# A gated recurrence in chunks: from seven levels of scores to one product with factored decays, the old way kept behind a branch

## The chip, the cores and the metric

The kernel runs on one core of one Trainium2 chip. Of the core's engines five appear in the profile: PE (TensorE: matrix products and transposes, with PEld for its weight loads), DVE (VectorE), ACT (ScalarE), POOL (GpSimd) and SP (SyncE, which issues the DMAs). The metric is the device time of one execution in microseconds. Before the change three timed executions took 1120.98 to 1123.78 us, median 1121.86.

## The reference

Two layers follow each other. The first is a gated linear recurrence, for 4 batches, 8 heads, 768 tokens and a head size of 48; the second mixes tokens through a rank of 32 and then channels through 1536 hidden ones.

```python
f = 1.0 / (1.0 + np.exp(-f_logit))
for t in range(S):
    state = f[:, :, t, :, None] * state + np.einsum('bhd,bhe->bhde', k[:, :, t], v[:, :, t])
    y[:, :, t] = np.einsum('bhd,bhde->bhe', q[:, :, t], state)
...
x = y.transpose(0, 2, 1, 3).reshape(B, S, H * D)
u = x + (x.transpose(0, 2, 1) @ U @ V).transpose(0, 2, 1)
out = u + np.maximum(u @ w_ch1, 0.0) @ w_ch2
```

Inputs q, k, v and f_logit are float32; f_logit is normal with mean 2 and deviation 0.5. The four weights arrive as float64 (their scale is a float64 number), and the kernel converts them to float32 on the chip from their bits.

## The kernel before, in words

Work goes in 16 *units*: a unit is two heads of one batch, one on partitions 0 to 47 and one on 64 to 111. The 768 tokens are cut into six chunks of 128. `attention(n, fill)` does a unit. PE transposes f, k and q (L182) so that channels lie on partitions and tokens along the free axis; ACT takes them out of PSUM, f with a sigmoid. Within a chunk the decay between two tokens is a product of f; it is built up in seven levels of a binary tree. On each level PE makes 12 score products `sc` of 64 columns (L231), DVE or ACT puts the part that belongs to the level into the score matrix A (L241 with a mask, L250 for the last two), DVE multiplies half of q (L253), POOL half of k (L256) by a neighbouring block's decay, and POOL forms the next level's block products (L261). The next level's scores wait for both. The diagonal comes from a product `dg` (L202). Then k is transposed back (L267), `ds` gives what each chunk adds to the state (L278), DVE runs the state from chunk to chunk (`st`, L286 and L288), and y is A times v plus q times state (L299, L301), copied by ACT into `x`.

`mixer(b)` makes a list of pieces for one batch: `low_rank` (`ph`, L317), six times `mix` (`pu` L324, the residual L325, and transposes `put` L331), and for each half of the tokens 12 times `ch1` (`pz`, L338, ReLU alternating between ACT and DVE) and three times `ch2` (`po`, L350, residual L353, and the store). The pieces of batch b are handed out as filler among the steps of the next batch's attention by `fill()`; those of the last batch stand alone at the end. During the first batch the filler is the weight conversion, `load_weight`, 32 tiles: a load into one of two `w_raw` buffers, one operation on ACT (L146), six on DVE (L147 to L153) and one on POOL (L154).

The program is recorded through a scheduler, which sets each engine's order by its own priorities; each engine then runs its list strictly in order, and so does SP's list of DMAs.

## Time and profile before

| | |
|---|---|
| timed executions | 1120.98, 1121.86, 1123.78 us |
| profiled execution, span from first to last instruction | 1124.9 us |
| own time of the profiled execution | given as the span alone; 1.1 us over the slowest timed one |
| PE busy | 1004.1 us, 89% |
| PEld / DVE / POOL / ACT busy | 726.0 / 334.8 / 266.0 / 144.2 us |
| batch 0 of attention, with the weight conversion | 0 to 252 us |
| batches 1, 2, 3, each with the mixer of the one before | 252 to 501, to 750, to 1003 us |
| last mixer, alone | 1003 to 1125 us |

In the group rows a name such as `sc<-qT,kT` is output and inputs by the program's tile names; behind it stand the shapes, the count of instructions, busy time, the mean in ns and the idle time before with what ended it. A float32 product on PE is two instructions. In timeline rows the first two numbers are the start and the length in us. The clock column is the TensorE clock that was granted, 1.00 being full.

### The profile page before, as it was taken

The page shows a single profiled execution, that of the slowest core. Times are in us where ns is not written, and L with a number is a line of the kernel's source. Part 1 is how long each engine was busy: PE and PEld are TensorE (multiplying, and loading weights), DVE is VectorE, ACT ScalarE, POOL GpSimd, SP SyncE. Part 2 cuts the span into 40 slices and gives each one's busy share as a digit, 9 for nine tenths or more (in the row PEclk, how much of TensorE's full clock was granted, in tenths as well). Part 3 has the DMA queues.
Part 4 walks back from the last instruction along what each step waited for, and adds up shares of the span by engine and source line. Part 5 has one row for each costly group of instructions (what it writes and reads, how often), then busy time and mean ns, then how long its engine had stood idle before and what let it go on. Part 6 is the DMA issues. An engine that isn't in the chain of part 4 may idle for free.

```text
span 1124.9 us, 13357 instructions
## 1 busy us (share of the span) xinstructions
PE 1004.1 (89%) x5592; PEld 726.0 (65%) x5592; DVE 334.8 (30%) x675; ACT 144.2 (13%) x269; POOL 266.0 (24%) x320
## 2 busy tenths in 40 slices
PE   5764748589999999999999999999999999988998
PEld 4654647576676767676766667576767667654555
DVE  3538585513223042213132142103132132101110
ACT  1111202011111111010111111010111111011000
POOL 4343533422131223022131223112131223100000
PEclk9999655556689898966689898965689998956999
DMA  9133423101030303010020302020020000000000
GB/s 129 29 82 85 99 70 76 38 11 32 1 43 1 56 8 43 15 39 11 1 43 8 57 1 43 22 43 1 1 43 8 15 1 1 22 1 0 8 15 21
DMA packets 108284, 34.29 MB, mean 30 GB/s; under 512 B 102016, under 2 KB 105088, under 8 KB 108224
## 3 DMA queue, kind: packets, MB, share of 16 engines
q1 hardware_dynamic: 108224, 33.44, 15.6%
q8 instruction: 44, 0.72, 0.3%
q14 instruction: 16, 0.13, 0.0%
HBM read 28.70 MB, written 4.72 MB: 30 GB/s over the span
## 4 chain that ended last, share of the span: by engine, by line
PE 81%; DVE 8%; POOL 6%; issue 3%; ACT 1%; POOLq 0%; DVEq 0%
PE sc L231 21%; PE po L350 17%; PE pz L338 14%; PE y L299 8%; PE y L301 7%; DVE A L241 5%; PE pt L182 4%; PE pu L324 3%; PE dg L202 2%; DVE qT L253 2%; POOL prod L261 2%; PE ph L317 2%; PE put L331 2%; POOL kT L256 2%; POOL qk L199 1%
## 5 line engine op out<-in xcount | busy, mean ns | idle before, releaser
L231 PEld LDWEIGHTS sc<-qT,kT 48*128 48x128 f32 x2688 | 226.2, 245 | 150.6 <-issue 91.1
L231 PE MATMUL sc<-qT,kT 48*128 48x64 f32 x2688 | 246.2, 336 | 86.0 <-DVE qT L253 63.0
L338 PE MATMUL pz<-uT,w 128*128 128x384 f32 x576 | 218.1, 524 | 0.8 <-ACT diag L205 0.8
L350 PE MATMUL po<-w,z 128*128 128x384 f32 x576 | 191.0, 489 | 0.0
L256 POOL TENSOR_TENSOR kT<-kT,prod 128x384 f32<-128x384 f32 x96 | 94.9, 989 | 356.6 <-PE sc L231 356.6
L241 DVE COPY_PREDICATED A<-mask,sc 128x384 f32<-128x384 int32 x160 | 110.6, 755 | 158.5 <-PE sc L231 157.4
L350 PEld LDWEIGHTS po<-w,z 128*128 128x128 f32 x576 | 108.4, 191 | 72.7 <-issue 0.3
L338 PEld LDWEIGHTS pz<-uT,w 128*128 128x128 f32 x576 | 110.0, 202 | 67.7 <-issue 9.8
L299 PE MATMUL y<-v_nat,A 128*128 128x48 f32 x384 | 99.9, 368 | 0.0
L301 PE MATMUL y<-st,qT 48*128 48x48 f32 x320 | 92.6, 381 | 0.3 <-DVE st L286 0.3
L299 PEld LDWEIGHTS y<-v_nat,A 128*128 128x128 f32 x384 | 78.8, 265 | 11.2
L301 PEld LDWEIGHTS y<-st,qT 48*128 48x128 f32 x320 | 68.7, 267 | 20.0 <-DVE st L288 4.9
L215 DVE TENSOR_TENSOR qT<-qT,fT 128x768 f32<-128x768 f32 x16 | 17.2, 1073 | 212.2 <-POOL qk L199 212.2
L253 DVE TENSOR_TENSOR qT<-qT,prod 128x384 f32<-128x384 f32 x96 | 55.4, 578 | 75.8 <-PE sc L231 75.8
L353 DVE TENSOR_TENSOR o<-x,po 128x384 f32<-128x384 f32 x24 | 13.3, 554 | 159.1 <-PE po L350 159.1
L209 POOL TENSOR_TENSOR A<-ident,diag 128x768 f32<-128x768 f32 x32 | 46.5, 1473 | 47.8 <-ACT diag L205 47.8
L261 POOL TENSOR_TENSOR prod<-fT 128x384 f32<-128x384 f32 x16 | 13.2, 826 | 183.2 <-ACT fT L190 180.0
L344 ACT ACTIVATE z<-pz 128x384 f32<-128x384 f32 x48 | 23.6, 491 | 240.3 <-PE pz L338 240.3
L250 ACT COPY A<-sc 32x384 f32<-32x384 f32 (+1 forms) x48 | 27.7, 577 | 189.5 <-PE sc L231 189.3
L342 DVE TENSOR_SCALAR z<-pz 128x384 f32<-128x384 f32 x48 | 26.6, 555 | 75.3 <-PE pz L338 75.3
L199 POOL TENSOR_TENSOR qk<-qT,kT 128x768 f32<-128x768 f32 x16 | 28.9, 1804 | 53.2 <-ACT qT L192 53.2
L202 PEld LDWEIGHTS dg<-halves,qk 128*128 128x128 f32 x192 | 27.8, 226 | 17.4 <-POOL qk L199 14.6
(57 smaller groups left out, 638.4 us busy)
## 6 DMA issues: line engine op xcount, KB each, us to landing
w_raw<-in_moe_w_ch_dram SPq DMA_DIRECT2D x24, 384.0 KB, 3.2
f_nat<-in_f_logit_dram SPq DMA_DIRECT2D x32, 144.0 KB, 3.0
k_nat<-in_k_dram SPq DMA_DIRECT2D x32, 144.0 KB, 3.4
q_nat<-in_q_dram SPq DMA_DIRECT2D x32, 144.0 KB, 3.9
v_nat<-in_v_dram SPq DMA_DIRECT2D x32, 144.0 KB, 3.8
out_dram<-o SPq DMA_DIRECT2D x24, 192.0 KB, 1.9
w_raw<-in_moe_U_dram SPq DMA_DIRECT2D x6, 32.0 KB, 1.7
w_raw<-in_moe_V_dram SPq DMA_DIRECT2D x2, 96.0 KB, 2.0
```

The costliest lines, as they stand in the source:

```text
L182: nc.tensor.transpose(pt[:, c // (NCH // 2), (c % (NCH // 2)) * C : (c % (NCH // 2) + 1) * C], nat[n % NSLOT][nm][:, c].rearrange("p h d - ...
L199: nc.gpsimd.tensor_tensor(qk, T["q"], T["k"], ALU.mult)
L202: nc.tensor.matmul(dg[:, 2 * c : 2 * c + 2], lhsT=qk[:, chunk[c]], rhs=halves, start=True, stop=True)
L209: nc.gpsimd.tensor_tensor(A[:, par], ident.unsqueeze(1).broadcast_to((P, NCH, C)), diag[:, :, par : par + 1].broadcast_to((P, NCH, C)), AL ...
L231: nc.tensor.matmul(sc[:, par, c * HC : (c + 1) * HC], lhsT=T["k"][r, chunk[c]], rhs=qv[r, c * nbc : (c + 1) * nbc, 1, :], start=True, stop ...
L241: nc.vector.copy_predicated(A[:, par].rearrange("p c (n two h) -> p (c n) two h", two=2, h=half)[:, :, 1, :], masks[l].unsqueeze(1).broadc ...
L253: nc.vector.tensor_tensor(qv[:, :, 1, :], qv[:, :, 1, :], bv[:, :, 0:1].broadcast_to((P, nb, half)), ALU.mult)
L256: nc.gpsimd.tensor_tensor(kv[:, :, 0, :], kv[:, :, 0, :], bv[:, :, 1:2].broadcast_to((P, nb, half)), ALU.mult)
L299: nc.tensor.matmul(o, lhsT=A[:, par, c, :], rhs=vt[:, c, par, :], start=True, stop=(c == 0))
L301: nc.tensor.matmul(o, lhsT=T["q"][r, chunk[c]], rhs=st[r, c, :], start=False, stop=True)
L338: nc.tensor.matmul(pm[:, 0:HALF], lhsT=w1[:, m, i * P : (i + 1) * P], rhs=uT[a][:, m, :], start=(m == 0), stop=(m == NDC - 1))
L350: nc.tensor.matmul(pm[:, 0:DM], lhsT=z[a, i][:, s * P : (s + 1) * P], rhs=w2[:, i, :], start=(i == 0), stop=(i == NFC - 1))
```

## The change

The kernel gets a new main path, `factored_path`, and keeps the old one as `general_path`, which runs behind a branch at the end when a flag says that the new one's range did not suffice.

The new path loads f, k and q so that a partition holds 24 tokens of 48 channels in one run of 1136 numbers, for 32 channels with some overlap, and turns 32 x 32 blocks on DVE. Decays are factored: X is the product of f from a token to the chunk's end (a scan backwards along the tokens), Y is the product from the chunk's start to a token divided by the whole chunk's (a scan forwards that begins each chunk with the reciprocal). k is multiplied by X and q by Y on POOL, so one score product of 128 columns for each chunk and head gives all pairs, and a causal mask on DVE takes them into A. `ds`, the states and y's state part are done for both heads in one product, with a mask `own` that clears what belongs to the other head. The smallest product of each chunk is kept, and the flag `ok` says whether all are at least 1e-18.

Work on a unit is cut in pieces: `attend(n)` (scores, kept, scores, states, read) and, interleaved with it, `prepare(n + 1)` (gates, keep, keys, read, queries), with filler after each. In the mixer a tile is now transposed (`turn`) after the next one's `mix`, and ReLU is on ACT alone. In the conversion ACT's operation is gone, and POOL has one more.

```diff
-        low, head, m = tmp(F32, "w_low"), tmp(U32, "w_head"), tmp(F32, "w_m")
-        nc.scalar.activation(low, lo, AF.Copy, scale=2.0**-52)
+        head, m = tmp(U32, "w_head"), tmp(F32, "w_m")
...
-        nc.vector.scalar_tensor_tensor(m, head, 2.0**-20, low, ALU.mult, ALU.add)
+        nc.vector.scalar_tensor_tensor(m, lo, 2.0**-32, head, ALU.mult, ALU.add)
...
+        nc.gpsimd.tensor_scalar(m, m, 2.0**-20, None, ALU.mult)
         nc.gpsimd.tensor_tensor(dst, m, s.bitcast(F32), ALU.mult)
...
-            if i % 2:
-                nc.vector.tensor_relu(out=z[a, i], in_=pm[:, 0:HALF])
-            else:
-                nc.scalar.activation(z[a, i], pm[:, 0:HALF], AF.Relu)
+        nc.scalar.activation(z[a, i], pm[:, 0:HALF], AF.Relu)
...
-        todo = [low_rank] + [lambda t=t: mix(t) for t in range(NCH)]
+    todo = [low_rank]
+    for t in range(NCH):
+        todo.append(lambda t=t: mix(t))
+        if t:
+            todo.append(lambda t=t: turn(t - 1))
+    todo.append(lambda: turn(NCH - 1))
...
+def factored_path(ctx, tc, q, k, v, f_logit, moe_U, moe_V, moe_w_ch1, moe_w_ch2, out, ok):
...
+    raw = [{nm: const.tile([P, W], F32, name=f"{nm}_raw{i}") for nm in "fkq"} for i in range(2)]
...
+                    nc.sync.dma_start(
+                        out=dst[p0 : p0 + rows, :],
+                        in_=bass.AP(head.tensor, head.offset + part * NB, [[TB * D, rows], [1, W]]),
+                    )
...
+    def turned(t, src_tile):
+        nc.vector.transpose(
+            t.rearrange("p (i c) -> p c i", c=TB),
+            bass.AP(src_tile.tensor, src_tile.offset, [list(src_tile.ap[0]), [D, TB], [1, NB]]),
+        )
...
+        def gates():
+            fT = one.tile([P, S], F32, name="fT")
+            turned(fT, r["f"])
+            fv = fT.rearrange("p (c t) -> p c t", t=C)
+            nc.scalar.activation(by_chunk[:, :, 1:C], fv[:, :, 1:C], AF.Sigmoid)
+            f0 = T["f0"] = two.tile([P, NCH], F32, name="f0")
+            nc.scalar.activation(f0, fv[:, :, 0], AF.Sigmoid)
+        def keep():
+            X = T["X"] = one.tile([P, S], F32, name="X")
+            nc.vector.tensor_tensor_scan(
+                backwards(X, S - 1, S), backwards(f, S, S), backwards(ends, S - 1, S), 0.0,
+                ALU.mult, ALU.add,
+            )
+            X0 = X.rearrange("p (c t) -> p c t", t=C)[:, :, 0]
+            nc.vector.tensor_copy(least[:, n, :], X0)
...
+            nc.vector.tensor_single_scalar(X1, X0, LEAST, ALU.max)
+            nc.vector.reciprocal(e.rearrange("p (c t) -> p c t", t=C)[:, :, 0], X1)
...
+            nc.vector.tensor_tensor(whole, T["f0"], X0, ALU.mult)
+        def keys():
...
+            turned(kT, r["k"])
+            nc.gpsimd.tensor_tensor(kT, kT, T["X"], ALU.mult)
+        def read():
...
+            nc.vector.tensor_tensor_scan(Y, f[:, 0:S], e, 0.0, ALU.mult, ALU.add)
+        def queries():
...
+            turned(qT, r["q"])
+            nc.gpsimd.tensor_tensor(qT, qT, T["Y"], ALU.mult)
+            if n + 2 < NU:
+                load_unit(n + 2)
...
+        def scores(g):
...
+            for c in range(G):
+                for par in range(2):
+                    nc.tensor.matmul(
+                        sc[:, par, c * C : (c + 1) * C],
+                        lhsT=T["k"][rows[par], chunk[g * G + c]],
+                        rhs=T["q"][rows[par], chunk[g * G + c]],
+                        start=True, stop=True,
+                    )
+            for par in range(2):
+                nc.vector.tensor_tensor(
+                    T["A"][:, par, g * G : (g + 1) * G, :],
+                    sc[:, par, 0 : G * C].rearrange("p (c i) -> p c i", i=C),
+                    causal.unsqueeze(1).broadcast_to((P, G, C)),
+                    ALU.mult,
+                )
...
+        def states():
...
+                nc.tensor.matmul(
+                    ds[:, c * PW : (c + 1) * PW], lhsT=T["kb"][:, c, :],
+                    rhs=vt[:, c].rearrange("p h d -> p (h d)"), start=True, stop=True,
+                )
...
+            nc.gpsimd.tensor_tensor(
+                st, dn, T["whole"][:, 1:NCH].unsqueeze(2).broadcast_to((P, NCH - 1, PW)), ALU.mult
+            )
+            for c in range(2, NCH):
+                nc.vector.scalar_tensor_tensor(
+                    st[:, c - 1, :], st[:, c - 2, :], T["whole"][:, c : c + 1], st[:, c - 1, :],
+                    ALU.mult, ALU.add,
+                )
...
+                if c:
+                    nc.tensor.matmul(o, lhsT=T["q"][:, chunk[c]], rhs=T["st"][:, c - 1, :],
+                                     start=True, stop=False, skip_group_check=True)
+                for par in range(2):
+                    nc.tensor.matmul(o[:, par * D : (par + 1) * D], lhsT=T["A"][:, par, c, :],
+                                     rhs=vt[:, c, par, :], start=(c == 0), stop=True,
+                                     skip_group_check=True)
...
+    nc.vector.tensor_single_scalar(ok, lowest, LEAST, ALU.is_ge)
+    for f in todo:
+        f()
...
+    good = nc.values_load(ok[0:1, 0:1], min_val=0, max_val=1)
+    with tc.If(good == 0):
+        with ExitStack() as inner:
+            general_path(inner, tc, *args)
```

The scheduler sets the order anew. PE, a unit of batch 0 before the change, from its scores to the first y with a state (names as in the section on the kernel before):

```order
L202 MATMUL dg<-halves,qk 128x2 x6
L231 MATMUL sc<-qT,kT 128x64 x84
L267 MATMUL pt<-ident,kT 128x128 x5
L299 MATMUL y<-v_nat,A 128x48 x3
L182 MATMUL pt<-ident,f_nat_122 128x128 x3
L278 MATMUL ds<-v_nat,kb 64x48 x10
```

The same on PE in the changed program, unit 0:

```order
L308 MATMUL sc<-qT,kT 128x128 x6
L325 MATMUL pt<-ident,kT 128x128 x5
L308 MATMUL sc<-qT,kT 128x128 x6
L334 MATMUL ds<-v_nat,kb 128x96 x5
L362 MATMUL y<-v_nat,A 128x48 x2
L359 MATMUL y<-st,qT 128x96
```

The scores went from 84 products to two groups of six, and the transposes of f, k and q and the diagonal have left PE.

DVE in the changed program, unit 3 of batch 0: masks into A (L315) and states (L349) among the weight conversion (L46 to L53), with the numbers of the tiles:

```order
L53 SCALAR_TENSOR_TENSOR w_s_423<-w_raw_415,w_e_421 128x384
L315 TENSOR_TENSOR A_924<-sc_925,causal_106 128x384
L48 SCALAR_TENSOR_TENSOR w_m_443<-w_raw_440,w_head_442 128x384
L50 TENSOR_SCALAR w_e_446<-w_raw_440 128x384
L315 TENSOR_TENSOR A_924<-sc_986,causal_106 128x384
L51 TENSOR_SCALAR w_e8_447<-w_e_446 128x384
L315 TENSOR_TENSOR A_924<-sc_986,causal_106 128x384
L52 TENSOR_SCALAR w_e_446<-w_e8_447 128x384
L339 TENSOR_TENSOR dn_1004<-ds_998,own_109 128x480
L53 SCALAR_TENSOR_TENSOR w_s_448<-w_raw_440,w_e_446 128x384
```

A mask that waits for PE now stands between two steps of a conversion; before, the level's mask L241 and the product L253 stood in such places, seven times a unit.

PE in the changed program, from the low-rank step of batch 0's mixer to unit 4's scores (ph L73, pu L80, put L89):

```order
L73 MATMUL ph<-x,U 32x384 x6
L80 MATMUL pu<-h,V 128x384 x2
L89 MATMUL put<-ident,x 128x128 x3
L80 MATMUL pu<-h,V 128x384
...
L80 MATMUL pu<-h,V 128x384
L308 MATMUL sc<-qT,kT 128x128 x6
L325 MATMUL pt<-ident,kT 128x128 x5
```

Units 0 to 3 stand ahead of it without filler on PE, since the filler of batch 0 is conversion; unit 4's scores stand behind most of the low-rank step, and batch 0's pz behind unit 4's.

More of the change, by code (lines that the diff above doesn't have):

```diff
@@ L346, in ch2 @@
-        def ch2(a, s):
-            t = a * TPH + s
-            pm = ps_mm.tile([P, 512], F32, name="po", tag="mm")
-            for i in range(NFC):
-                nc.tensor.matmul(pm[:, 0:DM], lhsT=z[a, i][:, s * P : (s + 1) * P], rhs=w2[:, i, :],
-                                 start=(i == 0), stop=(i == NFC - 1))
-            o = three.tile([P, DM], F32, name="o")
-            nc.vector.tensor_tensor(o, x[:, t, :], pm[:, 0:DM], ALU.add)
-            nc.sync.dma_start(out=out[b, t * P : (t + 1) * P, :], in_=o)
@@ L356, in mixer @@
-        todo = [low_rank] + [lambda t=t: mix(t) for t in range(NCH)]
-        for a in range(2):
-            todo += [lambda a=a, i=i: ch1(a, i) for i in range(NFC)]
-            todo += [lambda a=a, s=s: ch2(a, s) for s in range(TPH)]
-        return todo
+        return mixer_pieces(nc, b, x_tiles[b], U, V, w1, w2, ident, out, two, three, zp, ps_mm)
     FILLS = NL + 3
@@ L380, with kernel @@
         f()
+@with_exitstack
+def kernel(
+    ctx: ExitStack,
+    tc: tile.TileContext,
+    q: bass.AP,
+    k: bass.AP,
+    v: bass.AP,
+    f_logit: bass.AP,
+    moe_U: bass.AP,
+    moe_V: bass.AP,
+    moe_w_ch1: bass.AP,
+    moe_w_ch2: bass.AP,
+    out: bass.AP,
+):
+    nc = tc.nc
+    args = (q, k, v, f_logit, moe_U, moe_V, moe_w_ch1, moe_w_ch2, out)
+    flag = ctx.enter_context(tc.tile_pool(name="flag", bufs=1))
+    ok = flag.tile([1, 1], I32, name="ok")
+    with ExitStack() as inner:
+        factored_path(inner, tc, *args, ok)
+    good = nc.values_load(ok[0:1, 0:1], min_val=0, max_val=1)
+    with tc.If(good == 0):
+        with ExitStack() as inner:
+            general_path(inner, tc, *args)
 _INS = ['q', 'k', 'v', 'f_logit', 'moe_U', 'moe_V', 'moe_w_ch1', 'moe_w_ch2']
```

302 lines of the change are left out of this document (241 added, 61 removed).

## The prediction

> **What bounds the kernel now.** I read the page's head first, then a table of five stretches (one for each batch of attention, and the last mixer), then the chain of waits.
>
> ```profile
> span 1124.9 us, 13357 instructions
> PE 1004.1 (89%) x5592; PEld 726.0 (65%) x5592; DVE 334.8 (30%) x675; ACT 144.2 (13%) x269; POOL 266.0 (24%) x320
> DVE  3538585513223042213132142103132132101110
> ```
> ```profile
> core 0: us, PE busy (x) PEld busy (x) DVE busy (x) ACT busy (x) POOL busy (x), PEclk, DMA share, GB/s
> 0.00:252.00 252.00, 164.99 (x1074) 148.20 (x1074) 134.35 (x303) 38.94 (x73) 96.14 (x123) 0.74 0.35 69
> 252.00:501.00 249.00, 240.52 (x1400) 170.97 (x1399) 62.30 (x116) 32.06 (x59) 57.46 (x68) 0.83 0.14 25
> 501.00:750.00 249.00, 240.70 (x1399) 170.97 (x1399) 62.47 (x116) 32.07 (x59) 57.46 (x68) 0.83 0.14 25
> 750.00:1003.00 253.00, 244.28 (x1393) 173.31 (x1393) 62.31 (x116) 31.82 (x59) 54.90 (x61) 0.81 0.07 14
> 1003.00:1125.00 122.00, 113.61 (x330) 62.59 (x330) 13.35 (x24) 9.31 (x20) 0.00 (x0) 0.91 0.03 10
> ```
> The last line of the head has DVE in 40 slices of 28 us. Two regimes. From 252 us on, PE is busy 97% of the time: what counts is its number of instructions. In the first 252 us nothing is full: PE and DVE take turns, with the weight conversion (DVE) between them. The chain says the same:
>
> ```profile
> by line: PE sc L231 20.8%; PE po L350 16.8%; PE pz L338 14.1%; PE y L299 7.6%; PE y L301 7.0%; DVE A L241 4.7%; PE pt L182 3.8%; issue 2.7%; PE pu L324 2.6%; PE dg L202 2.5%; DVE qT L253 1.9%; POOL prod L261 1.8%; PE ph L317 1.7%; PE put L3
> ```
> Scores, y, dg and pt, that is attention, hold most of PE's part; the mixer's pz and po come next. The prices on PE (a float32 product counts as two instructions, a transpose as one):
>
> ```profile
> L231 PE MATMUL sc<-qT,kT 48*128 48x64 f32 x2688 | 246.2, 336 | 86.0 <-DVE qT L253 63.0 <-POOL kT L256 16.7 <-DVE w_head L147 5.0
> L338 PE MATMUL pz<-uT,w 128*128 128x384 f32 x576 | 218.1, 524 | 0.8 <-ACT diag L205 0.8
> L350 PE MATMUL po<-w,z 128*128 128x384 f32 x576 | 191.0, 489 | 0.0
> L324 PE MATMUL pu<-h,V 32*128 32x384 f32 x48 | 35.7, 841 | 0.6 <-ACT h L320 0.6
> L331 PE MATMUL put<-ident,x 128*128 128x128 f32 x72 | 20.8, 423 | 4.3 <-DVE x L325 4.3
> L317 PE MATMUL ph<-x,U 128*32 128x384 f32 x48 | 19.8, 570 | 0.7 <-ACT x L304 0.7
> L267 PE MATMUL pt<-ident,kT 128*128 128x128 f32 x80 | 16.2, 351 | 9.4 <-POOL kT L256 9.4
> L278 PE MATMUL ds<-v_nat,kb 128*64 128x48 f32 x320 | 16.3, 263 | 0.0
> ```
> I use busy time over count, not the mean: the records overlap. The mixer is 218.1 + 191.0 + 35.7 + 20.8 + 19.8 = 485.4 us of PE and is kept. In the middle batches it takes 121 of 249 us, so attention takes 128, or 32 per unit. The change works on those 32.
>
> **The change, part by part.** Gone are seven levels of scores with their masks and waits, the diagonal, and 18 transposes per unit on PE. Now PE does per unit 12 score products, 5 transposes, 5 ds products and 17 for y. DVE takes over transposes and gains two scans. So the first stretch becomes DVE's, the rest stays PE's, and I sum the two apart.
>
> *Stage 1, DVE, until unit 5's last state.* The order shows why it ends there: PE's scores for units 4 and 5 stand behind DVE's transposes, which stand among the conversions; the last conversions lie between unit 5's states.
>
> ```profile
> L353 DVE TENSOR_TENSOR o<-x,po 128x384 f32<-128x384 f32 x24 | 13.3, 554 | 159.1 <-PE po L350 159.1
> L215 DVE TENSOR_TENSOR qT<-qT,fT 128x768 f32<-128x768 f32 x16 | 17.2, 1073 | 212.2 <-POOL qk L199 212.2
> L288 DVE SCALAR_TENSOR_TENSOR st<-st,prod,ds 128x48 f32<-128x48 f32 x64 | 16.8, 263 | 2.0
> L147 DVE TENSOR_SCALAR w_head<-w_raw 128x384 uint32<-128x384 uint32 (+2 forms) x32 | 13.1, 408 | 3.1 <-DMA w_raw<-in_moe_w_ch_dram 3.0
> L148 DVE SCALAR_TENSOR_TENSOR w_m<-w_head,w_low 128x384 f32<-128x384 uint32 (+2 forms) x32 | 15.5, 486 | 4.0 <-POOL w L154 2.2 <-ACT w_low L146 1.3 <-POOL U L154 0.3
> L150 DVE TENSOR_SCALAR w_e<-w_raw 128x384 uint32<-128x384 uint32 (+2 forms) x32 | 18.3, 573 | 0.1
> L151 DVE TENSOR_SCALAR w_e<-w_e 128x384 uint32<-128x384 uint32 (+2 forms) x32 | 12.2, 382 | 0.3
> L152 DVE TENSOR_SCALAR w_e<-w_e 128x384 uint32<-128x384 uint32 (+2 forms) x32 | 11.0, 343 | 0.4
> L153 DVE SCALAR_TENSOR_TENSOR w_s<-w_raw,w_e 128x384 uint32<-128x384 uint32 (+2 forms) x32 | 19.8, 620 | 0.5
> L152 DVE TENSOR_SCALAR w_e<-w_e 128x32 uint32<-128x32 uint32 x6 | 1.1, 181 | 0.2
> ```
> Conversion: 13.1 + 15.5 + 18.3 + 12.2 + 11.0 + 19.8 = 89.9 us. A unit: four score masks of 384 from PSUM at 0.554 (L353's shape), 2.22; one of 480, 0.69; four state steps at 0.263, 1.05; four operations on six numbers at 0.18, what 32 numbers cost in the last row, 0.72. Neither a 32x32 transpose nor a scan is in the trace. The nearest row has the same 768 elements, L215 at 1.07. A transpose I bound by ACT's 768-wide copy (0.80, below) and twice 1.07, and take 1.07. A scan has two inputs as L215 has, and each output needs the one before: 1.07 to 2.15, and I take the middle, 1.6. Unit: 4.68 + 3 x 1.07 + 2 x 1.6 = 11.1 us (9.2 to 15.4); six units 67.
>
> [...]
>
> Between, DVE waits:
>
> ```profile
> 4.66 1.51 PE L182 MATMUL pt<-ident,f_nat 128*128 128x128 f32 x6 [4.66 <-DVE mask_f L85]
> 39.52 2.83 PE L231 MATMUL sc<-qT,kT 48*128 48x64 f32 x24 [1.67 <-DVE w_head L147]
> 47.88 1.33 PE L267 MATMUL pt<-ident,kT 128*128 128x128 f32 x5 [1.35 <-POOL kT L256]
> ```
> ```profile
> L199 POOL TENSOR_TENSOR qk<-qT,kT 128x768 f32<-128x768 f32 x16 | 28.9, 1804 | 53.2 <-ACT qT L192 53.2
> L192 ACT COPY kT<-pt 128x768 f32<-128x768 f32 x16 | 12.8, 799 | 26.6 <-PE pt L182 26.6
> w_raw<-in_moe_w_ch_dram SPq DMA_DIRECT2D x24, 384.0 KB, 3.2
> ```
> The first gates land at about 5 us (4.66 before, for half the bytes). From the last query transpose to the first mask DVE waits for POOL's product (1.8) and six score products on a cold PE (12 instructions, 1.4 at 2.83 / 24, more for twice the columns: 2.1); the second half then waits for five transposes and six products less two masks (1.33 + 2.1 - 1.1); ds about 0.8: 7 us. Units 0 to 2 have little conversion to fill it: 21 us. In units 3 to 5 conversions stand in the gaps, but a mask row waits in order with conversions queued behind it: 4 each, 12. On SP a w_raw load waits for one of two buffers, and the next unit's inputs stand behind it; it lands in 3.2 us, about one conversion: 5 us of waits. The residual adds: 6 x 0.55 = 3.3. **Stage 1: 5 + 67 + 90 + 21 + 12 + 5 + 3 = 203 us.**
>
> *Stage 2, PE.* In stage 1 PE has done ph, pu and put of one batch (76.3 / 4 = 19) and 24 of 288 pz products (18): 485.4 - 37 = 448 us are left, the exposed last mixer included. Ten units are left.
>
> ```profile
> 486.03 1.35 PE L299 MATMUL y<-v_nat,A 128*128 128x48 f32 x6
> 560.37 0.66 PE L299 MATMUL y<-v_nat,A 128*128 128x48 f32 x2
> 603.56 0.77 PE L299 MATMUL y<-v_nat,A 128*128 128x48 f32 x6
> ```
> Scores: 24 instructions between L231's 246.2 / 2688 = 0.092 and twice that for twice the columns: 2.2 to 4.4, middle 3.3. Transposes 16.2 / 16 = 1.0. Ds: half the instructions, each twice as wide both ways: from 16.3 / 16 = 1.0 to ten at the slow 128-row price above (1.35 / 6 = 0.225), 2.3; middle 1.7. y: 34 instructions, all on 128 rows. Alternating with 48-row products one costs 0.33 on a slow clock (0.66 for two); in a run of their own 0.225, or 0.77 / 6 = 0.13 fast. Nearest is the fast run, since pz stands around it: 0.145, 4.9 in all. **Unit 10.9 (8.6 to 19), ten units 109.**
>
> Waits: the level-to-level stalls (86 us at L231) have nothing left to wait for. What is late next is y, for the states: ds 1, DVE's 0.7, POOL's 480 of 768 elements at 1.8, and four steps of 0.26, together 4 us, while three to nine pz products (0.64 each, below) cover 2 to 6. I leave 1 us a unit, 10; behind a late y stand PE's next pz, and nobody waits for those but ACT. The last mixer idles 122.0 - 113.6 = 8.4; turning a tile after the next mix takes off some 3: 5. ReLU, now all on ACT, hides under the 1.9 us of products that make a tile; uncovered it costs 0.4 a tile (half of L192's 768). The input loads double in bytes but are issued a unit ahead, and hide under that unit's 11 us of DVE or more; uncovered, a landing is 3 to 4 us. At the end each engine loads the flag and jumps over the other path: 0 to 10 (three landings of 3.2), and I take 4, near one.
>
> **Sum: 203 + 448 + 109 + 15 + 4 = 779 us** against the profiled span of 1124.9; the median, 1121.86, lies 3 below it, so 776.
>
> **The rivals.**
> - *PE stays fast* (0.22). pz and po carry slow stretches: the last mixer's run shows the price without them.
>
> ```profile
> 1051.81 23.38 PE L350 MATMUL po<-w,z 128*128 128x384 f32 x72
> 560.00:566.00 6.00, 6.00 (x22) 5.09 (x22) 0.00 (x0) 0.00 (x0) 0.00 (x0) 0.50 0.00 0
> ```
>  72 instructions in 23.2 us is 0.3225 each, 371.5 for 1152 against 409.1. The clock halves in the long y runs (0.50 at 560); shorter ones may not reach it. Saved: 36 on pz and po, 23 with units at 8.6, 11 on DVE with 9.2, and half of stage 1's waits, 16: 690. Against it: ph and pu remain. [...]
> - *DVE is dearer* (0.17). Transposes and scans at 2.15 give 15.4 a unit, 26 more; w_raw waits that nothing hides, 1.6 (half of 3.2) for each of 24 tiles, 38: 840. For it: six new large operations without a row; against: DVE before waited only 3.1 for such loads.
> - *PE stays slow in attention* (0.06): 19 a unit, 81 more, and pz and po lose their 38 twice: 895. The 0.50 at 560 speaks for it, the 0.8 of every stage above against it.
> - *The other path runs too* (0.02). If a product of 127 gates falls below 1e-18, the whole old program follows: 776 + 1122 = 1898, slower. Worked out from the reference's inputs the smallest is 7.9e-10, so only a fault in the flag would do it; then the change would not do what it says either.
>
> **How the numbers follow.** Forecast 0.53, rivals 0.22, 0.17, 0.06, 0.02. The range, 690 to 855, holds the forecast's own bounds, most of the dearer-DVE case and the slower half of the fast one; 0.2 stays outside. Below 0.3% (3.4 us) this measurement tells nothing apart. Only the last rival is not faster: faster 0.97, same 0.01, slower 0.02.
>
> **What would show it.** Stage 1: DVE near 80% busy up to about 200 us, a unit's own work near 11 us, scans at 1.6. Stage 2: PE over 95% busy, a y run of 17 products near 5 us, middle batches of about 165 us. The end: 122 us or a little less from the last x to the end, then under 10 us of jumps. Wrong, if PE waits for DVE after 250 us, if one scan or transpose costs over 2.2, or if L536 appears.

## The result, and the profile after

The changed kernel takes 722.62 us (median of four runs, 721.53 to 724.5); the kernel before, timed beside it, 1122.82. The ratio is 0.6434, with an interval of 0.6413 to 0.6455: 1.55 times as fast. The forecast was 776 us, 53 above the time; the range of 690 to 855 holds it.

The head of the page after, with DVE's 40 slices (now of 18 us each):

```profile
span 719.6 us, 6593 instructions
PE 614.4 (85%) x2489; PEld 403.6 (56%) x2489; DVE 336.6 (47%) x539; ACT 98.1 (14%) x205; POOL 143.5 (20%) x123
DVE  6668798999984566254553542354211201000000
```

PE has lost 390 of its 1004 us, 200 of them at the scores (`sc` has 45.9 us, L231 had 246.2); DVE has lost none. The table of stretches, cut where unit 5's last y product ends and where the last sum ends (columns as before the change: length, then busy time and count of PE, PEld, DVE, ACT and POOL, the granted clock, the DMA share and GB/s):

```profile
0.00:211.00 211.00, 116.25 (x527) 91.31 (x528) 173.80 (x316) 22.64 (x47) 97.39 (x93) 0.85 0.49 117
211.00:713.00 502.00, 498.16 (x1964) 312.26 (x1963) 162.41 (x224) 75.48 (x158) 46.12 (x30) 0.94 0.19 45
713.00:719.00 6.00, 0.00 (x0) 0.00 (x0) 0.36 (x1) 0.00 (x0) 0.00 (x0) 0.80 0.11 38
```

The two stages are there as forecast: DVE busy 82% of the first 211 us, PE 99% of the rest, and then some 6 us of end. What differs is the price of the second stage, which its groups show (first the 211 to 713 us of PE alone, then three of DVE's dearest over the whole run):

```profile
L105 PE MATMUL po<-w,z 128*128 128x384 f32 x576 | 188.7, 487 | 0.0
L96 PE MATMUL pz<-uT,w 128*128 128x384 f32 x528 | 182.0, 498 | 0.0
L362 PE MATMUL y<-v_nat,A 128*128 128x48 f32 x243 | 39.3, 289 | 0.0
L308 PE MATMUL sc<-qT,kT 48*128 48x128 f32 x240 | 26.1, 325 | 0.0
L80 PE MATMUL pu<-h,V 32*128 32x384 f32 x36 | 22.8, 737 | 0.8 <-ACT h L76 0.6 <-DVE x L81 0.2
L89 PE MATMUL put<-ident,x 128*128 128x128 f32 x54 | 14.8, 400 | 2.1 <-DVE x L81 2.1
L73 PE MATMUL ph<-x,U 128*32 128x384 f32 x36 | 12.1, 487 | 0.6 <-DVE o L108 0.6
```
```profile
L237 DVE STREAM_TRANSPOSE fT<-f_raw 128x768 f32<-128x768 f32 x16 | 33.3, 2079 | 6.4 <-DMA f_raw<-in_f_logit_dram 4.4 <-DMA out_dram<-o 1.9
L261 DVE TENSOR_TENSOR_SCAN X<-fz,ends 128x768 f32<-128x768 f32 x16 | 28.1, 1757 | 26.0 <-ACT fz L255 20.4 <-ACT f L257 5.3
L48 DVE SCALAR_TENSOR_TENSOR w_m<-w_raw,w_head 128x384 f32<-128x384 uint32 (+2 forms) x32 | 21.8, 680 | 2.5 <-POOL w L55 2.2 <-POOL U L55 0.2
```

The mixer's five lines take 188.7 + 182.0 + 22.8 + 14.8 + 12.1 = 420.4 us of the second stage; what is left of PE's 498.2 is attention: 77.8 us, 7.8 for each of ten units. (Records overlap where one product follows another; here the overlap is counted with the mixer.) One unit's y run, from the timeline (start, length):

```profile
251.72 0.54 PE L362 MATMUL y<-v_nat,A 128*128 128x48 f32 x4
252.09 0.43 PE L359 MATMUL y<-st,qT 128*128 128x96 f32 x2
252.36 0.57 PE L362 MATMUL y<-v_nat,A 128*128 128x48 f32 x4
...
255.44 4.10 PE L96 MATMUL pz<-uT,w 128*128 128x384 f32 x12
```

From the first y to the next pz pass 3.72 us: 0.11 for each of the 34 instructions, at a granted clock of 1.00.

### The profile page after: what moved, and what is told of

It is laid out like the page before. It is cut to its first block, busy times and chain, and to the rows that moved or that the text cites. A ratio compares the mean times of both kernels' runs of the same rounds, so it can differ in the third digit from the quotient of the medians.

```text
span 719.6 us, 6593 instructions
## 1 busy us (share of the span) xinstructions
PE 614.4 (85%) x2489; PEld 403.6 (56%) x2489; DVE 336.6 (47%) x539; ACT 98.1 (14%) x205; POOL 143.5 (20%) x123
## 4 chain that ended last, share of the span: by engine, by line
PE 76%; DVE 14%; DMA 3%; issue 3%; POOL 2%; ACT 1%; SPq 1%; DVEq 0%; ACTq 0%; POOLq 0%
PE pz L96 25%; PE po L105 25%; PE sc L308 5%; PE y L362 5%; PE ds L334 4%; PE y L359 3%; PE pu L80 3%; PE ph L73 2%; DMA w_raw<-in_moe_w_ch_dram 2%; DVE kT L237 2%; PE put L89 2%; PE pt L325 2%; DVE w_m L48 2%; DVE X L261 1%; DVE fT L237 1%
## 5 line engine op out<-in xcount | busy, mean ns | idle before, releaser
L96 PE MATMUL pz<-uT,w 128*128 128x384 f32 x576 | 200.9, 502 | 0.0
L105 PE MATMUL po<-w,z 128*128 128x384 f32 x576 | 188.7, 487 | 0.0
L308 PE MATMUL sc<-qT,kT 48*128 48x128 f32 x384 | 45.9, 370 | 86.9 <-POOL qT L285 86.9
L308 PEld LDWEIGHTS sc<-qT,kT 48*128 48x128 f32 x384 | 35.5, 252 | 105.2 <-POOL qT L285 89.2
L276 POOL TENSOR_TENSOR kT<-kT,X 128x768 f32<-128x768 f32 x16 | 30.3, 1894 | 200.0 <-DVE kT L237 187.9
L315 DVE TENSOR_TENSOR A<-sc,causal 128x384 f32<-128x384 f32 x64 | 33.2, 551 | 63.6 <-PE sc L308 63.5
L359 PE MATMUL y<-st,qT 128*128 128x96 f32 x160 | 42.9, 359 | 4.8 <-POOL st L345 4.8
L237 DVE STREAM_TRANSPOSE qT<-q_raw 128x768 f32<-128x768 f32 x16 | 33.5, 2094 | 18.7 <-PE y L359 18.7
L54 POOL TENSOR_SCALAR w_m<-w_m 128x384 f32<-128x384 f32 (+2 forms) x32 | 34.4, 1074 | 36.4 <-DVE w_m L48 23.4
L359 PEld LDWEIGHTS y<-st,qT 128*128 128x128 f32 x160 | 32.7, 251 | 7.2 <-POOL st L345 5.9
L237 DVE STREAM_TRANSPOSE fT<-f_raw 128x768 f32<-128x768 f32 x16 | 33.3, 2079 | 6.4 <-DMA f_raw<-in_f_logit_dram 4.4
L237 DVE STREAM_TRANSPOSE kT<-k_raw 128x768 f32<-128x768 f32 x16 | 33.2, 2074 | 0.0
L80 PE MATMUL pu<-h,V 32*128 32x384 f32 x48 | 30.1, 731 | 3.1 <-ACT uT L91 1.7
```

The lines of the kernel that those rows point to most:

```text
L54: nc.gpsimd.tensor_scalar(m, m, 2.0**-20, None, ALU.mult)
L80: nc.tensor.matmul(pm[:, 0:DM], lhsT=V[:, t * P : (t + 1) * P], rhs=h[0], start=True, stop=True)
L96: nc.tensor.matmul(pm[:, 0:HALF], lhsT=w1[:, m, i * P : (i + 1) * P], rhs=uT[a][:, m, :], start=(m == 0), stop=(m == NDC - 1))
L105: nc.tensor.matmul(pm[:, 0:DM], lhsT=z[a, i][:, s * P : (s + 1) * P], rhs=w2[:, i, :], start=(i == 0), stop=(i == NFC - 1))
L237: nc.vector.transpose(t.rearrange("p (i c) -> p c i", c=TB), bass.AP(src_tile.tensor, src_tile.offset, [list(src_tile.ap[0]), [D, TB], [1, ...
L276: nc.gpsimd.tensor_tensor(kT, kT, T["X"], ALU.mult)
```

## The experiments

Every kernel was timed beside the kernel before, on the same chip, and its ratio is to that one.

**Where y's price comes from: two kernels.** In the changed kernel the state part of y is one product for both heads, on 128 rows. Both kernels do it head by head, on 48 rows, 10 products in place of 5. In the first each follows its A product, as in the kernel before.

```diff
-                if c:
-                    nc.tensor.matmul(o, lhsT=T["q"][:, chunk[c]], rhs=T["st"][:, c - 1, :],
-                                     start=True, stop=False, skip_group_check=True)
                 for par in range(2):
...
+                    o = y[:, par, c * D : (c + 1) * D]
+                    nc.tensor.matmul(o, lhsT=T["A"][:, par, c, :], rhs=vt[:, c, par, :],
+                                     start=True, stop=(c == 0))
+                    if c:
+                        nc.tensor.matmul(o, lhsT=T["q"][rows[par], chunk[c]],
+                                         rhs=T["st"][rows[par], c - 1, par * D : (par + 1) * D],
+                                         start=False, stop=True)
```

> The changed kernel (722.6 us), but y's state part as it was before: per chunk and head one product over the head's 48 rows, alternating with the 128-row product of A (10 more instructions per unit than in the changed kernel, 44 for 34). Theory (alternation costs): PE pays 0.35 us per pair in such a run instead of 0.20 to 0.27, y per unit goes from 3.7 to 7.3 us at full clock, 36 us for the ten units that lie on PE's path, and the clock drops in the longer run, 10 to 25 more: 765 to 785 us, granted clock under 0.90. Rival (only the count of instructions matters): 10 more at 0.13 in ten units, 13 us: 735 us, clock as it was (0.91).

In the second the same products stand in two groups, all of A and then all of the states. In it the two parts of y are not added as in the reference, so its result is not the reference's; its products are the same in shape and number.

> The same products and the same count as in the run with alternation, but grouped: first all twelve 128-row products of A, then all ten 48-row products with the state, so there is one switch of rows per unit instead of twenty. Theory (alternation costs): most of that run's loss is gone, 718 to 735 us, and y takes 3 to 4.5 us per unit. Rival (count of instructions, or the smaller rows themselves): as slow as the run with alternation.

Measured: 817.52 us alternating (813.39 to 819.5; ratio 0.7265, interval 0.7227 to 0.7302), 32 above the range of its theory, and 738.14 grouped (733.04 to 740.24; ratio 0.6553, interval 0.6514 to 0.6591), 3 above. The same products in another order cost 79 us. The timelines of one y run, first alternating, then grouped:

```profile
272.41 0.42 PE L362 MATMUL y<-st,qT 48*128 48x48 f32 x2
272.75 0.42 PE L359 MATMUL y<-v_nat,A 128*128 128x48 f32 x2
...
275.44 0.66 PE L362 MATMUL y<-st,qT 48*128 48x48 f32 x2
276.04 0.66 PE L359 MATMUL y<-v_nat,A 128*128 128x48 f32 x2
```
```profile
254.67 2.77 PE L358 MATMUL y<-v_nat,A 128*128 128x48 f32 x24
257.37 1.35 PE L363 MATMUL y<-st,qT 48*128 48x48 f32 x20
```

Alternating, a product of two instructions goes every 0.35 us, and from 274.86 us on, 3.2 us into the run that began at 271.71, every 0.59: the granted clock is 0.50 there, for 10.2 us, the last three of them over the pz behind the run. The run lasts 10.2 us. Grouped, 24 instructions take 2.70 and 20 take 1.28 us, 4.0 in all, with the clock at 1.00 up to 258.5. So what the forecast took for y's slow price is the change of rows from product to product and the clock that falls in such a run, not 48 columns or the count. At the full clock a product takes 0.35 us in turn, 0.22 (2.70 / 12) and 0.13 (1.28 / 10) in groups; what in the change of rows costs the difference no run here shows. The spell at the half clock lasts 10.2 us in each of the eight y runs of the second stage that begin at the full clock.

The grouped kernel is still 15 us above the changed one, with a y run only 0.3 us longer. Between 230 and 560 us its granted clock is at the half for some 75 us instead of 51, which is 12 us (from one `pz` instruction to the next pass 0.32 us at 1.00 and 0.64 at 0.50 in the changed kernel); ten units of 0.3 make the rest. The further spells are five, of 3.4 or 6.8 us, and each begins 3.3 to 4.4 us after the start of a y run (the first at 258.5 us, for the run at 254.67 above). In the changed kernel, with y on 128 rows alone, none of the eight y runs that begin at the full clock has such a spell. So the clock falls with products on 48 rows in a group too: the price of 0.35 comes from the order, but that the change of rows, and not the few rows themselves, brings the clock down isn't shown.

**The mixer's rows.** The same alternation stands in the mixer: `pu` on 32 rows between `put` on 128. V and h get rows of zeros up to 128; nothing else changes.

```diff
-        h[0] = two.tile([R, DM], F32, name="h")
-        nc.scalar.copy(h[0], pm[0:R, 0:DM])
+        h[0] = hz if hz is not None else two.tile([R, DM], F32, name="h")
+        nc.scalar.copy(h[0][0:R, :], pm[0:R, 0:DM])
...
-    V = const.tile([R, S], F32, name="V")
+    V = const.tile([P, S], F32, name="V")
+    hz = const.tile([P, DM], F32, name="hz")
+    nc.gpsimd.memset(V, 0.0)
+    nc.gpsimd.memset(hz, 0.0)
```

> V and h are filled with rows of zeros from 32 to 128, so that the mix products run on 128 rows as the transposes beside them do; the count of instructions, their columns and the result stay. Theory of the rows (what slows PE is the alternation of products on few rows with products on 128, as with y on 48 rows): a mix product goes from 0.63 us (30.1 / 48) to the 0.33 of a ph product at the full clock, 14 us; put goes from 0.27 to 0.19, 6 us; together 14 to 20 us less, 703 to 709 us. Rival (the granted clock falls in the mixes for another reason, such as the load of the stretch before, and 128 rows of which 96 are zeros load PE no less): within 3 us of the changed kernel.

It ran beside the changed kernel itself, once more:

> The changed kernel once more, unaltered, beside the three that follow, so that differences of a few us are read against a time of the same chip. All theories: 721 to 725 us.

Measured: 722.68 us for the changed kernel (ratio 0.6419, interval 0.64 to 0.6438), 706.77 with the zeros (705.59 to 711.91; ratio 0.6282, interval 0.626 to 0.6304): 16 less. The last mixer from ph to pz in this repeated run of the changed kernel, and the same place with the zeros:

```profile
604.59 4.03 PE L73 MATMUL ph<-x,U 128*32 128x384 f32 x12 [0.63 <-DVE o L108]
609.18 1.55 PE L80 MATMUL pu<-h,V 32*128 32x384 f32 x4 [0.56 <-ACT h L76]
...
611.38 1.64 PE L80 MATMUL pu<-h,V 32*128 32x384 f32 x2
612.95 0.90 PE L89 MATMUL put<-ident,x 128*128 128x128 f32 x3
...
621.64 18.66 PE L96 MATMUL pz<-uT,w 128*128 128x384 f32 x52
```
```profile
593.68 4.03 PE L73 MATMUL ph<-x,U 128*32 128x384 f32 x12 [0.63 <-DVE o L108]
598.26 1.56 PE L80 MATMUL pu<-hz,V 128*128 128x384 f32 x4 [0.56 <-ACT hz L76]
...
603.59 0.91 PE L80 MATMUL pu<-hz,V 128*128 128x384 f32 x2 [0.32 <-DVE x L81]
604.33 0.49 PE L89 MATMUL put<-ident,x 128*128 128x128 f32 x3
...
607.09 23.39 PE L96 MATMUL pz<-uT,w 128*128 128x384 f32 x72
```

A `pu` goes from 1.57 us to 0.75, a `put` from 0.83 to 0.49, and from ph to pz pass 13.4 us instead of 17.05 (16.1 in the first profile of the changed kernel), though PE now waits for DVE's sums. Most of this is the clock. It is at 0.50 in the first timeline from 611.3 us on, for 13.7 us, and at 1.00 in the whole of the second. At the full clock two `pu` in a row take 1.55 us on 32 rows and 1.56 on 128; one that a `put` follows takes 0.84 (609.03 to 609.87 in the first profile) and 0.75. In all eleven profiles of the changed kernel and its variants with `pu` on 32 rows the clock falls in the last mixer, for 10 to 17 us; in the two with zeros, this one and the last of this section, it does not. Three quarters of the rows are zeros, 96 of 128, and it is still the faster form.

The rest of the gain lies between 230 and 560 us, where ph, pu and put stand at the seams between batches: the clock is at the half there for 24 us, and for 51 and 55 in the two profiles of the changed kernel. There the rows are not shown to be the cause, since a kernel with `pu` on 32 rows has 24 as well (the one that turns at once, below).

**DVE's transposes in the first stage.** Units 0 to 5 are loaded with the tokens on partitions, PE turns them and ACT carries them out; units 6 to 15 stay on DVE. With `NPE = 6`, and f and q in the same way as k:

```diff
-            turned(kT, r["k"])
+            if n < NPE:
+                nc.scalar.copy(kT.rearrange("p (a t) -> p a t", a=2), on_pe(n, "k")[:, :, 0 : G * C])
+            else:
+                turned(kT, r["k"])
```

> The changed kernel, but for units 0 to 5, those of the first stage, f, k and q are loaded as before the change and transposed on PE, with ACT taking them out of PSUM; units 6 to 15 stay on DVE's transposes. Theory (DVE's own work sets the first stage): 18 transposes of 2.08 us leave DVE there, 37 us, and PE has room for its 108 transposes: 680 to 695 us; PE's first products of unit 5 start at about 160 instead of 196 us. Rival (the chain DVE, POOL, PE sets the stage, or the w_raw loads): under 12 us gained, 710 to 722.

Measured: 687.99 us (685.49 to 688.26; ratio 0.6114, interval 0.6088 to 0.6141), 35 less. The 18 transposes of these units are 18 x 2.08 = 37 us of DVE: in the first stage its work is worth its time almost one to one. PE had 146 us behind it at 200 us instead of 105, only 21 of them for the added transposes.

**And in the second stage?** All 16 units' transposes go to PE.

> The transposes of all 16 units, and not only of the first six, are done by PE with ACT carrying them out of PSUM; DVE transposes nothing. Theory of the two stages (from unit 6 on PE sets the time and DVE's transposes are hidden): ten units times 18 transposes at 0.13 to 0.2 us are 23 to 35 us more than with six units on PE, 711 to 723 us against 688. Rival (PE waits for DVE in the second stage too): within 5 us of 688.

Measured: 684.66 us (684.31 to 686.11; ratio 0.6085, interval 0.6071 to 0.6099). The theory fell, and the rival held only by its number: PE does 26 us more (47.5 for all `ptr`, the transposes of f, k and q, against 21.2 for six units), and nothing is lost. Two places in the second stage show why: the seams between batches, with ph, pu and put. The changed kernel first, where ph starts at 304.7 and 455.4 us, then the one with all transposes on PE, where it starts at 275.0 and 421.1:

```profile
310.00:350.00 40.00, 37.86 (x141) 25.31 (x140) 16.35 (x25) 7.20 (x16) 4.57 (x3) 0.66 0.34 77
450.00:490.00 40.00, 40.00 (x153) 25.70 (x152) 18.89 (x28) 6.06 (x13) 4.56 (x3) 0.70 0.11 31
```
```profile
280.00:320.00 40.00, 39.11 (x229) 27.15 (x227) 17.59 (x34) 12.93 (x28) 7.40 (x5) 1.00 0.24 45
416.00:456.00 40.00, 39.10 (x215) 24.45 (x214) 17.23 (x32) 10.67 (x25) 4.62 (x3) 1.00 0.18 35
```

In stretches of 2 us the changed kernel's clock reads 1.00 or 0.50 there, and something between only where it changes (0.95 at 312, 0.72 at 340), so a mean of 0.66 over 40 us is 27 us at the half, and 0.70 is 24: 51 us between 230 and 560, all in two spells that begin in these seams. With six units on PE it is 48 us, with all on PE none. 48 us at the half are 24 us at the full clock, with the prices of `pz` above, about what the added transposes cost. Why the clock then stays up isn't shown: `pu` still stands on 32 rows there.

**Turning at once, and fewer pieces.** In the first kernel `turn(t)` follows `mix(t)` directly, in one piece. In the second it stays one mix later, but as one piece with that mix. A mixer then has 37 and 38 pieces; the changed kernel has 43 for 40 places, so that some places take two. The first kernel's edit (the second pairs `mix(t)` with `turn(t - 1)`):

```diff
     for t in range(NCH):
-        todo.append(lambda t=t: mix(t))
-        if t:
-            todo.append(lambda t=t: turn(t - 1))
-    todo.append(lambda: turn(NCH - 1))
+        todo.append(lambda t=t: (mix(t), turn(t)))
```

> A tile is turned straight after its own mix again, as in the kernel before, so that PE's transposes wait for DVE's sum. The theory of the prediction (turning a tile after the next mix takes 3 us off the last mixer, the only place where nothing else fills PE): 3 us more, 725 to 727 us. Rival (the wait is there, but the mix stage with its slow clock loses nothing that PE had not lost): within 1 us of the changed kernel. Second rival (the seams of the three middle mixers lose as much each, since several pieces of them are issued in a row): 8 to 12 us more.

> Turning a tile stands again one mix later, as in the changed kernel, but as one piece with that mix: a mixer has 38 pieces for the 40 places beside attention, as turning at once had 37, where the changed kernel has 43. Theory of the pieces (turning at once gained 4.8 us because no place takes two pieces and the products are spread otherwise, and lost 4.7 us of them in the last mixer, where PE waits 0.7 us for each sum): both gains together, 712 to 715 us. Rival (turning late is itself what costs in the middle batches): 721 to 725 us, as the changed kernel.

Measured: 717.87 us for the first (711.6 to 720.72; ratio 0.6381, interval 0.6362 to 0.6401), 5 less than the changed kernel, where all three expectations had it equal or slower; and 711.71 for the second, whose runs lie far apart, 706.11 to 722.4 (ratio 0.6304, interval 0.627 to 0.6339, from the three up to 714.1). In the last mixer turning at once costs what the prediction said and more; the timeline of the first kernel has a wait of this kind six times:

```profile
586.83 4.06 PE L73 MATMUL ph<-x,U 128*32 128x384 f32 x12 [0.62 <-ACT x L364]
...
595.95 1.64 PE L80 MATMUL pu<-h,V 32*128 32x384 f32 x2
598.33 0.87 PE L89 MATMUL put<-ident,x 128*128 128x128 f32 x3 [0.74 <-DVE x L81]
...
608.55 24.75 PE L96 MATMUL pz<-uT,w 128*128 128x384 f32 x72
```

ph to pz takes 21.7 us, 4.7 more than in the repeated run of the changed kernel. But by then it is 18 us ahead of that run; the two profiles are of the fastest execution here and the slowest there, and the medians lie 5 apart. In the profile the half clock lasts 24 us between 230 and 560 instead of 55, and PE's idle time at the scores is 76.9 us instead of 87.6. The second kernel's profile is of its slowest execution, 722.4, and has 55 us at the half like the changed kernel. Both kernels with fewer pieces gained in the median, which points to the pieces and not to the order of turning; how the seams' clock depends on where the fillers fall isn't shown.

**The idle time of stage 1.** The weight loads go to ACT's queue, so that the next units' inputs on SP no longer stand behind them and conversions can fill DVE's gaps from the start.

```diff
-    load = weight_loader(nc, two, one, nc.sync)
+    load = weight_loader(nc, two, one, nc.scalar)
```

> The changed kernel with the weight loads issued on ACT's queue instead of SP's, where they stood behind three units' inputs; the scheduler then places the first conversions among units 0 to 2. Theory (idle of DVE in units 0 to 2, about 8 us each, is lost because no conversion is there yet): 15 to 24 us gained, 700 to 708 us. Rival (ACT's queue waits for w_raw buffers and holds back the sigmoids behind): no gain or a loss, 720 to 740 us.

Measured: 723.7 us (721.11 to 723.88; ratio 0.6432, interval 0.6404 to 0.6459): nothing gained. DVE's first 50 us fill up, and the waits turn up behind it (two rows of stretches, two of the waits up to 215 us):

```profile
0.00:50.00 50.00, 14.29 (x73) 13.19 (x73) 43.75 (x103) 4.55 (x8) 25.18 (x36) 1.00 0.55 125
150.00:200.00 50.00, 39.04 (x166) 25.66 (x167) 31.87 (x45) 7.99 (x18) 15.94 (x10) 0.93 0.61 127
```
```profile
PE sc L308 <- POOL qT L285: 79.1, 4, 30.6
ACT kb L329 <- DMA w_raw<-in_moe_w_ch_dram: 42.6, 2, 22.0
```

The conversions now stand ahead of the units' own steps in DVE's list: the first scores start at 30.59 us, and ACT, which issues the loads in order, holds `kb` for 42.6 us behind them, which is the rival's case. At 200 us DVE has done 171.6 us of work (164.4 in the changed kernel), but PE 90 instead of 105. Filling the engine that sets the time gained nothing, because what filled it stood in front of what others wait for.

**The conversion.** ACT scales the low word again as before the change; POOL's scaling is gone.

```diff
-        head, m = tmp(U32, "w_head"), tmp(F32, "w_m")
+        low, head, m = tmp(F32, "w_low"), tmp(U32, "w_head"), tmp(F32, "w_m")
+        nc.scalar.activation(low, lo, AF.Copy, scale=2.0**-52)
...
-        nc.gpsimd.tensor_scalar(m, m, 2.0**-20, None, ALU.mult)
```

> A weight tile is converted as in the kernel before: ACT scales the low word, DVE adds the high one, and POOL's extra scaling (32 operations, 34.3 us in all) is gone; the count of DVE's operations is the same. Theory of contention (DVE's conversion grew from 89.9 to 98 us because POOL works beside it; POOL's extra operations are half of that work): DVE's conversion falls back to 90 to 93 us, the first stretch ends 5 to 8 us earlier, 714 to 718 us. Rival (the growth comes from POOL's work for the units, which stays): 721 to 725 us. Second rival (ACT's step stands in front of DVE's sum and is late, as it was for 1.3 us before): 724 to 730 us.

Measured: 718.96 us (717.98 to 721.16; ratio 0.639, interval 0.6372 to 0.6408), some 3 us less and at the edge of what these intervals part. DVE's six operations take 96.4 us (25.0 + 18.8 + 15.9 + 15.6 + 10.9 + 10.2), against 97.7 in the repeated run of the changed kernel. So POOL's scaling isn't what made the conversion dearer, and the first theory fell. DVE waited 6.4 us for ACT's `w_low`, as the second rival has it, without a loss in the time. The median record of each operation is as long as before the change (0.35 us with one input, 0.55 with two); what some records take beyond it adds up to 25.7 us in the changed kernel, 23.9 here and 17.9 before the change. The two engines' timelines side by side in the changed kernel, DVE and then POOL, show such records:

```profile
128.20 0.59 DVE L53 SCALAR_TENSOR_TENSOR w_s<-w_raw,w_e 128x384 uint32<-128x384 uint32 x1
128.72 1.95 DVE L46 TENSOR_SCALAR w_head<-w_raw 128x384 uint32<-128x384 uint32 x1
130.60 1.14 DVE L50 TENSOR_SCALAR w_e<-w_raw 128x384 uint32<-128x384 uint32 x1
```
```profile
128.56 1.90 POOL L276 TENSOR_TENSOR kT<-kT,X 128x768 f32<-128x768 f32 x1 [1.79 <-DVE kT L237]
130.42 1.10 POOL L55 TENSOR_TENSOR w<-w_m,w_s 128x384 f32<-128x384 f32 x1
```

An operation that takes 0.35 us elsewhere starts just after a POOL product of two inputs and ends 0.2 us after it: at 130.67 behind 130.46, at 131.74 behind 131.52. In the changed kernel 18 records of 128 x 384 on L46, L50, L51 and L52 start within a two-input product of POOL that has 0.4 us or more to go. Sixteen of them end 0.22 us after that product; the two others, at 90.60 and 117.81 us, take 0.34 and 0.35. What holds DVE in the sixteen isn't shown. The products are those for k and q, the one for the states and the last one of a conversion, and all are still there without the scaling. That all of the long records come from this isn't shown: no run leaves those products out.

**The branch.** The flag is computed, but its load, the branch and the path behind it are left out; the fallback for gates too small is missing in this kernel.

> The flag is still computed, but nobody loads it, and the branch and the other path behind it are gone. The theory of the prediction (each engine loads the flag and jumps, about 4 us; the traces show 2.7 us from the last sum to the end of the span before and 6.2 after): 3 to 4 us less, 718.5 to 720 us. Rival (the end is the last store's landing, and the jumps hide beside it): no difference within 1 us. Second rival (the program's size costs time during the run, by the loading of its instructions): over 8 us less.

Measured: 719.13 us (717.94 to 719.79; ratio 0.6389, interval 0.6371 to 0.6406), 3.55 less than the changed kernel beside it. From the end of the last sum to the end of the span pass 6.2 us in the changed kernel (713.35 to 719.6) and 2.95 without the branch (713.05 to 716.0); before the change it was 2.7.

**Three edits together:** six units on PE, V and h on 128 rows, and turn and mix in one piece, one mix apart.

> Three edits together: the first six units' transposes on PE, V and h on 128 rows, and the turning of a tile as one piece with the next mix. Theory (the three act at different places: DVE in the first stretch, PE's mixes, the distribution of the pieces): 688 less 16 less 4 to 9, 663 to 668 us. Rival (the slow clock only moves to another place, since PE is busier): 675 to 685 us.

Measured: 659.14 us (658.82 to 660.01; ratio 0.5855, interval 0.5843 to 0.5868), 4 us below what its theory expected of the three, and 1.096 times as fast as the changed kernel, with the branch and the fallback in place. From 230 us to the last product its clock never falls.

## Why the prediction was right, and where its terms were off

The direction, the two stages and their limits are as the prediction put them, and so are most of its marks: DVE 82% busy up to 211 us, PE 99% from there on, 3 us of waits for DVE after that (2.1 of them for one sum at 313.5 us), 117.4 us from the last `ph` to the end (602.24 to 719.6), no second path. Three marks missed: a y run took 3.7 us and not near 5, a middle batch 147 to 151 us and not about 165, and a unit's own work on DVE some 15 us and not near 11 (transposes 6.2, scans 3.5, masks 2.2, states and small operations 2.9). The terms, in us of the profiled span:

| term | predicted | measured |
|---|---|---|
| stage 1, until unit 5's y | 203 | 211 |
| of it DVE busy (67 + 90 + 3) | 160 | 173.8 |
| of it DVE idle | 43 | 37.2 |
| mixer's products left | 448 | 420.4 |
| ten units on PE | 109 | 77.8 |
| waits and the last sum's tail | 15 | 3.8 + 3.1 |
| branch | 4 | 3.5 |
| sum | 779 | 719.6 |

- **A unit on PE, 10.9 us: mis-sized, and it measured 7.8**, below the low bound of 8.6. Every part was too dear. At the full clock, from the start of a group to the start of the next, y takes 3.7 us (put at 4.9), the two score groups 0.86 each, 1.7 (3.3), ds 1.1 (1.7) and the transposes 0.6 (1.0): 7.1 in all, and two of the ten units fall into spells at the half. For y the choice "nearest is the fast run", 0.145 an instruction, was too dear; it is 0.11 (3.72 / 34). The rows that it was bounded by came from products that alternate with 48-row ones, and the two y kernels show that alternation, which the change takes out, made both the long run and its dear products. Without it the slow end of the range has no place: grouped, the same A products go at 0.11 (2.70 / 24) too. For the scores, the larger part of the miss, 0.072 an instruction is below even the 0.092 that was taken as the lowest price, a mean over a run whose granted clock was 0.815; no run here tests them apart.
- **The mixer, 448 us: mis-sized by 27.6.** The prediction kept pz and po at the price that they had between the old kernel's long attention runs, 409.1 / 1152 = 0.355, and made a faster clock a rival. In stage 2 they cost (188.7 + 182.0) / 1104 = 0.336, a little more than half the way to the rival's 0.3225. That what stands beside pz and po sets their price is shown by the alternating kernel: with 48-row products back in y, pz and po rise by 21 us (216.7 + 193.7 against 200.9 + 188.7), since the half clock of a y run lasts into the pz behind it (3 of its 10.2 us in the run above). "PE stays fast" was half true, by its mechanism; "PE stays slow in attention" was false.
- **What the prediction missed is where the clock would still fall.** It counted ph and pu against the fast rival only as a remark. The padded V and h are worth 16 us, and in the second stage the half clock begins in those seams.
- **Transposes at 1.07: mis-sized.** They take 2.08, the upper bound, with 1.87 from start to start. The scans took 1.76, inside 1.07 to 2.15. The conversion took 97.7 instead of 89.9 (DVE's records overlap, by 0.07 in the rows of the conversion above, and its busy time grew by 14 and not by the 28 that these prices give). Idle time was 6 less than reckoned (the "cold PE" of its waits shows in the rows: from the first to the last start of a y run pass 8.25 us at 26.36, 46.85 and 67.47 us and 3.62 at 251.72, with 1.00 in the clock column in both; why isn't shown): stage 1 came out only 8 off because two errors went against each other, which is luck. "DVE is dearer" was right on transposes alone; of its 38 us of waits for weights there was a tenth: in the repeated run DVE waited 3.9 us for `w_raw` at L46.
- **Waits, 15: mis-sized.** Late states, put at 1 us a unit, cost nothing in stage 2: no y there waits. No product waits for ACT's ReLU either, as forecast.
- **The branch, 4: right** (3.5). **Turning later, "some 3" in the last mixer: right in its place** (4.7), but the prediction took it alone. Later turning also made 43 pieces of 37, and the kernel that undoes both was 5 us faster, so they cost more elsewhere than the 4.7 gained there.

The errors of the first stage (+8) and of the second (-67) have opposite signs. The second comes from one mistake for the most part: products were priced by rows with other neighbours and a lower clock. For y, pz, po and pu the kernels above show that; for the scores it is argued.

## What to carry to other kernels

A price per product from a profile held here only for its neighbourhood and for the clock granted there (y's products on 48 and 128 rows: 0.35 us in turn, 0.59 at the half clock, 0.18 in groups): see whether the row comes from a run of like products or from an alternation of 128 rows with fewer, and if it is the second, group the products or pad the operand with zeros (16 us here) before counting instructions. Where one engine sets the time of a stage and another that of the next, move work to the one that idles in that stage alone, as the six units' transposes did for 35 us. A gap on the limiting engine is not filled for free if the filler stands ahead of what other engines wait for: with the weight loads on ACT's queue `kb` waited 42.6 us, and the time was 723.7 us against 722.62.

## What the runs showed of the hardware that was not expected

- Products on 48 and 128 rows in turn cost 0.35 us each, twice the mean of 0.18 in groups. The granted clock halves 3.0 to 4.5 us after the start of such a run, for 10.2 us, and they cost 0.59 then. Grouped, it halves in or just behind six of eight runs, for 3.4 or 6.8 us; on 128 rows alone in none of eight.
- Zeros can be cheaper than few rows: beside `put`, a `pu` on 128 rows, 96 of them zeros, took 0.75 us; one on 32 rows took 0.84, and 1.57 after the granted clock had halved, as it did in every last mixer with 32 rows and in none with 128.
- A 128 x 768 float32 transpose of 32 x 32 blocks takes 2.08 us on DVE with these access patterns, twice a two-input product of that size (1.07 before the change) and more than a scan (1.76). Whether the turning or the strided pattern costs it, no run here parts.
- Of 18 DVE operations that take 0.35 us elsewhere and start within a two-input product on POOL with 0.4 us or more to go, 16 last until 0.22 us after its end: 1.14 us behind one of 1.10, 1.95 behind one of 1.90. The profile counts all of it as busy time.
